# Second tap sums of a short convolution: from GpSimd's adder to adding transfers

## The chip, the cores and the metric

The kernel runs on one core of a Trainium2 chip. The metric is the device time of one execution in microseconds, the lower the better. The median of three runs before the change is 163.78 us (163.3 to 164.11).

## The reference

Two independent blocks are computed on sequences of 2048 positions and 576 channels, all in bf16, and their outputs are put side by side. Block A is a short convolution with four taps along the sequence, a product with `v`, a long convolution (by FFT) and a product with `q`. Block B is linear attention with 32 heads.

```python
def _A_ref(q, k, v, shift_k, ssm_k, ssm_D):
    B, S, D = q.shape
    ks = shift_k.shape[-1]                     # 4
    k_pad = jnp.pad(k, ((0, 0), (ks - 1, 0), (0, 0)))
    k_shift = jnp.zeros_like(k)
    for t in range(ks):
        k_shift = k_shift + k_pad[:, t:t + S, :] * shift_k[:, ks - 1 - t][None, None, :]
    kv = k_shift * v
    ...                                        # y = causal convolution of kv with ssm_k, by FFT
    y = y + kv * ssm_D[None, None, :]
    return q * y

def _B_ref(x, wqkv, wo):
    ...                                        # q, k, v = split of x @ wqkv into 32 heads of 18
    phi = lambda t: jnp.where(t > 0, t + 1, jnp.exp(t)) + 1e-6
    pq, pk = phi(q), phi(k)
    kv = jnp.einsum("bhsd,bhse->bhde", pk, v)
    z = jnp.einsum("bhsd->bhd", pk)
    num = jnp.einsum("bhqd,bhde->bhqe", pq, kv)
    den = jnp.einsum("bhqd,bhd->bhq", pq, z)[..., None] + 1e-6
    ...                                        # (num / den) merged over the heads, @ wo
```

## The kernel before

The long convolution is a discrete Fourier transform done in two stages of matrix products (`s1`, line 456, with the table `Gsb`; a 32x32 block transpose on VectorE, line 495; `s2`, line 504), a product in the frequency domain, and two stages back (lines 540 and 565). In block B, `kproj` (lines 604 to 612) and `qproj` (lines 625 to 631) project x and apply phi, with the results `pk` and `pqT`; line 654 forms x's product with `pk` over all positions, and line 794 makes the output.

The work around the change is the short convolution, `conv_piece`. Positions lie as 128 partitions of 16 consecutive positions; a piece is one third of the channels (192, `cc` = 0, 1, 2) and one half of the 16 positions (`bh` = 0, 1). So there are six pieces, in the order in which the program lists them: first all of what needs the first half of k, `kh0` (and v, `v0`), then the second half. For each piece a tile `m` of 128 x 4 x 8 x 192 elements is filled and folded:

- two tap products on VectorE (line 395), each making two of the four taps: 128 x 3072 elements, k times the tap weights `Wj`;
- the first tap sum, always on VectorE in this plan: m[0:2] += m[2:4], 128 x 3072 elements;
- the second tap sum, m[0] += m[1], 128 x 1536 elements;
- the product with v, written over v: 128 x 1536 elements.

The sums and the product go through the helper `tt`, so all have line 234 in the profile.

Nothing is scheduled at run time. The program's operations are listed once with their data dependences, and then issued in the order that a long string, `PLAN`, writes out; its letter names the engine of each operation (P TensorE, A ScalarE, D VectorE, G GpSimd, S the transfer queue of SyncE). A second string, `PLACES`, gives the place of every buffer in SBUF and PSUM, and buffers that are dead lend their places to others. Each engine runs its instructions in order; waits between engines follow from the buffers' places and the data. In this plan GpSimd has four of the six second tap sums, and behind the first two of them the product with v as well; VectorE has the other two sums and four products. Operations marked `two` that are given to GpSimd also wait for the last one of VectorE so marked:

```python
            if o.info.get("two"):
                if o.eng == "DVE":
                    last = ins
                elif last is not None:
                    tc.add_manual_dep(ins, last.name, ...,
                                      reason="products of VectorE and GpSimd one after the other")
```

The third piece writes its `m` where the second piece's was. The second half of k is loaded (1584 KB, SyncE's queue) once the last tap product that reads the first half is done. After each group of x the kernel makes a narrow copy `x<-x_sb` (line 231 on GpSimd, 229 on VectorE, 227 on ScalarE).

The prediction also speaks of three transfers of SyncE's queue (line 220): `X<-sph`, 256 KB from SBUF to SBUF for the product in the frequency domain; `r_scr<-rden`, 64 KB of reciprocal denominators into HBM; and `rb<-r_scr`, which reads them back, spread over partitions.

## Time and profile before

| | |
|---|---|
| runs before, median (lowest to highest) | 163.78 us (163.3 to 164.11) |
| the profiled execution, its time | 163.43 us |
| its span, from the first to the last instruction | 161.7 us |
| TensorE clock granted, mean | 0.997 |
| TensorE matmul busy | 153.7 us (95%) |
| VectorE busy | 145.1 us (90%) |
| ScalarE busy | 125.9 us (78%) |
| GpSimd busy | 55.9 us (35%) |
| second tap sums on GpSimd | 4 of 3.1 us, 12.4 us |
| second tap sums on VectorE | 2 of 0.96 us |

Busy time is the time in which at least one instruction of the engine was being worked on. In the profile PE is TensorE, DVE is VectorE, ACT is ScalarE, POOL is GpSimd, and SPq is SyncE's queue of transfers. The slices are 40 equal parts of the span, 4.04 us each, and a digit is the busy share in tenths. The chain that ended last is followed back from the last instruction, at each step to what released it. "Idle before" in a timeline is how long the engine had stood still, and what ended that. In the table of windows the columns are the stretch, its length, the busy time of PE, PEld (weight loads), DVE, ACT and POOL with the number of instructions, the granted clock, the mean busy share of the 16 transfer engines and the GB/s that they moved.

### The profile page before, as it was taken

What the parts mean: (1) busy time and instruction counts of PE and PEld (TensorE: products, weight loads), DVE (VectorE), ACT (ScalarE), POOL (GpSimd) and SP (SyncE); (2) the same over time, 40 slices, a digit from 0 to 9 for tenths busy, and PEclk for the clock granted to TensorE, in tenths of its full rate; (3) what the DMA queues carried; (4) which work ended last, traced back from release to release, by engine and by line L of the source; (5) the groups of instructions that cost most, each with busy time, mean ns of one, the idle gap of its engine ahead of it and who ended that gap; (6) DMA issues with size and microseconds to landing.
All of it is one profiled execution on the core that took longest, in us unless ns stands there. A gap on an engine that the chain in (4) does not pass through costs nothing.

```text
span 161.7 us, 4161 instructions
## 1 busy us (share of the span) xinstructions
PE 153.7 (95%) x1671; PEld 119.6 (74%) x1671; DVE 145.1 (90%) x173; ACT 125.9 (78%) x231; POOL 55.9 (35%) x50
## 2 busy tenths in 40 slices
PE   6899989999999999998999999999999999999991
PEld 2687877644645587896878887887578799999991
DVE  1319999997999999999999999999999999999790
ACT  3139989998988968878645469997999999989512
POOL 8603411110079277051001600999960000002900
PEclk9999999999999999999999999999999999999998
DMA  5999999999930800284940044489996597122975
GB/s 166 288 402 244 232 124 160 309 293 271 401 132 0 292 4 0 41 348 94 334 174 4 18 166 167 158 312 287 299 352 270 155 383 247 65 70 71 264 194 175
DMA packets 25135, 32.20 MB, mean 199 GB/s; under 512 B 15387, under 2 KB 20508, under 8 KB 24348
## 3 DMA queue, kind: packets, MB, share of 16 engines
q1 hardware_dynamic: 25116, 31.94, 65.6%
q8 instruction: 13, 0.21, 0.6%
q14 instruction: 6, 0.05, 0.1%
HBM read 20.27 MB, written 4.98 MB: 156 GB/s over the span
## 4 chain that ended last, share of the span: by engine, by line
PE 57%; DVE 17%; DMA 9%; ACT 5%; SPq 4%; POOL 4%; issue 3%; DVEq 0%; ACTq 0%
PE ps_all L794 13%; PE ps_all L540 10%; PE ps_all L625 10%; PE ps_all L654 6%; PE ps_all L456 6%; PE ps_all L565 5%; DMA hs<-in_A_ssm_k_dram 4%; PE ps_all L504 4%; DVE m L395 4%; DMA kh<-in_A_k_dram 4%; SPq L322 2%; DVE Ch L229 2%; DVE ct L495 2%; DVE rden L742 2%; DVE Cu L229 2%
## 5 line engine op out<-in xcount | busy, mean ns | idle before, releaser
L234 POOL TENSOR_TENSOR m<-m 128x1536 bf16<-128x1536 bf16 x4 | 12.4, 3102 | 34.7 <-DVE m L234 30.7
L625 PE MATMUL ps_all<-xT,wq 128*126 128x512 bf16 (+1 forms) x100 | 24.2, 380 | 0.0
L234 POOL TENSOR_TENSOR pqT<-pqT,rb 126x1024 bf16<-126x1024 bf16 (+1 forms) x9 | 18.9, 2125 | 9.5 <-DVE v L234 9.5
L794 PE MATMUL ps_all<-M,pqT 126*128 126x288 bf16 (+1 forms) x160 | 21.8, 286 | 0.3 <-DVE M L782 0.3
L604 PE MATMUL ps_all<-wk,xT 128*128 128x288 bf16 x160 | 20.7, 286 | 0.6 <-DMA wk<-in_B_wqkv_dram 0.6
L395 DVE TENSOR_TENSOR m<-kh,Wj 128x3072 bf16<-128x3072 bf16 x12 | 20.7, 1767 | 0.3 <-POOL v L234 0.2
L604 PEld LDWEIGHTS <-xT 128*128 128x128 bf16 x160 | 17.3, 110 | 4.0 <-issue 1.5
L456 PEld LDWEIGHTS <-Gsb 128*128 128x128 bf16 x192 | 16.1, 98 | 5.0 <-issue 2.8
L794 PEld LDWEIGHTS <-pqT 126*128 126x128 bf16 (+1 forms) x160 | 16.8, 109 | 3.7 <-issue 1.8
L227 ACT ACTIVATE sph<-ps_all 128x512 bf16<-128x512 f32 x30 | 16.6, 602 | 2.4 <-PE ps_all L504 2.3
L625 PEld LDWEIGHTS <-wq 128*126 128x126 bf16 (+1 forms) x100 | 12.4, 131 | 7.8 <-issue 1.8
L227 ACT ACTIVATE Cu<-ps_all 128x768 bf16<-128x768 f32 x20 | 16.2, 861 | 1.6 <-DVE m L395 0.8
L540 PE MATMUL ps_all<-Esb,sph 128*128 128x128 bf16 x144 | 17.2, 219 | 0.0
L540 PE MATMUL ps_all<-Esb,X 128*128 128x128 bf16 x144 | 17.1, 219 | 0.0
L654 PE MATMUL ps_all<-pk,x_sb 128*128 128x289 bf16 (+1 forms) x128 | 16.8, 287 | 0.0
L227 ACT ACTIVATE V<-ps_all 128x512 bf16<-128x512 f32 x26 | 14.9, 641 | 2.3 <-PE ps_all L540 2.1
L227 ACT ACTIVATE spu<-ps_all 128x512 bf16<-128x512 f32 x28 | 15.4, 619 | 0.6 <-PE ps_all L504 0.6
L609 ACT ACTIVATE ek<-ps_all,neg 128x576 bf16<-128x576 f32 x16 | 11.8, 747 | 4.4 <-PE ps_all L604 3.4
L227 ACT ACTIVATE Ch<-ps_all 128x768 bf16<-128x768 f32 x18 | 14.8, 853 | 0.5 <-PE ps_all L456 0.2
L227 ACT ACTIVATE ob<-ps_all 128x288 bf16<-128x288 f32 x30 | 11.7, 437 | 4.5 <-PE ps_all L794 4.0
L234 POOL TENSOR_TENSOR q<-yb,q 128x768 bf16<-128x768 bf16 x3 | 4.9, 1652 | 28.8 <-PE ps_all L565 28.8
L654 PEld LDWEIGHTS <-x_sb 128*128 128x128 bf16 x128 | 12.4, 98 | 3.0
(94 smaller groups left out, 313.3 us busy)
## 6 DMA issues: line engine op xcount, KB each, us to landing
X<-sph SPq DMA_DIRECT2D x18, 256.0 KB
x_sb<-in_B_x_dram SPq DMA_DIRECT2D x4, 576.0 KB
v<-in_A_v_dram SPq DMA_DIRECT2D x2, 1152.0 KB
out_dram<-ob SPq DMA_DIRECT2D x16, 144.0 KB
q<-in_A_q_dram SPq DMA_DIRECT2D x1, 2304.0 KB
out_dram<-q SPq DMA_DIRECT2D x12, 192.0 KB
rb<-r_scr SPq DMA_DIRECT2D x8, 252.0 KB
kh<-in_A_k_dram SPq DMA_DIRECT2D x1, 1584.0 KB
```

Source lines behind the costliest of these rows:

```text
L227: nc.scalar.activation(out=o, in_=i, func=ACTF.Copy)
L229: nc.vector.tensor_copy(out=o, in_=i)
L234: return (nc.vector if e == "DVE" else nc.gpsimd).tensor_tensor(out=o, in0=a, in1=b, op=op)
L395: return nc.vector.tensor_tensor(out=m.t[:, i:i + 2], in0=i0, in1=i1, op=ALU.mult)
L456: nc.tensor.matmul(ps.t[:, bank, lo - 384 * bank:hi - 384 * bank], lhsT=Gsb.t[:, b, ri, :], rhs=src[:, lo - CC * j:hi - CC * j], start=Tru ...
L540: nc.tensor.matmul(ps.t[:, 0, 128 * c:128 * c + 128], lhsT=src.t[:, 4 * hh + c, :], rhs=Esb.t[:, 32 + wi, :], start=(wi == 0), stop=(wi == 1))
L565: nc.tensor.matmul(ps.t[:, 0, n * j:n * j + n], lhsT=Esb.t[:, 2 * b + ri, :], rhs=V[gi].t[:, 2 * b + ri, :], start=(ri == 0), stop=(ri == 1))
L604: nc.tensor.matmul(ps.t[:, hh, 0:HALF], lhsT=cols(xT.t[0:KT[t], t, :], r), rhs=wk.t[0:KT[t], t, HALF * hh:HALF * hh + HALF], start=(t == 0 ...
L609: P.op("A", lambda e: nc.scalar.activation(out=eb.t[:], in_=ps.t[:, :, 0:HALF], func=ACTF.Exp, bias=neg1.t[:]), rd=[ps, neg1], wr=[eb], na ...
L625: nc.tensor.matmul(ps.t[0:hn, 0, :], lhsT=wq.t[0:KT[t], t, h0:h0 + hn], rhs=xT.t[0:KT[t], t, :], start=(t == 0), stop=(t == 4))
L654: nc.tensor.matmul(ps.t[0:m, 0, 0:n], lhsT=x4[r // 4].t[:, r % 4, :] if t == 4 else x_sb[r // 4].t[:, r % 4, 128 * t:128 * t + 128], rhs=p ...
L794: nc.tensor.matmul(ps.t[:, 0, 0:HALF], lhsT=cols(pqT[r // 8].t[0:kn, c, 512 * (r // 4 % 2):512 * (r // 4 % 2) + 512], r), rhs=M.t[0:kn, c, ...
```

## The change

The second tap sum of a piece that the plan gives to GpSimd is no longer an addition on GpSimd, but a transfer issued from GpSimd's queue, which reads m[1] from SBUF and adds it to m[0] in SBUF. The sums that the plan gives to VectorE stay as they are. `PLAN` and `PLACES` are unchanged, so every engine has the same operations in the same order, and each buffer lies where it lay.

```diff
-        P.op("DG", lambda e: tt(e, m.t[:, 0], m.t[:, 0], m.t[:, 1], ALU.add),
+        def add2(e):
+            if e == "POOL":
+                return nc.gpsimd.dma_start(out=m.t[:, 0].rearrange("p a c -> p (a c)"), in_=m.t[:, 1].rearrange("p a c -> p (a c)"), accum_op=ALU.add)
+            return tt(e, m.t[:, 0], m.t[:, 0], m.t[:, 1], ALU.add)
+        P.op("DG", add2,
              wr=[(m, 0)], name="tap+", n=1536, x2=1, two=1, st=st)
```

What waited for the addition now waits for the transfer's landing: GpSimd's product with v for the first two, VectorE's for the last two, and whatever takes the place of m.

## The prediction

> **What bounds the kernel now.** I read the busy table first, then the slices, the chain that ended last, and last the timelines of the engines around the four sums.

> ```profile
> span 161.7 us, 4161 instructions
> PE 153.7 (95%) x1671; PEld 119.6 (74%) x1671; DVE 145.1 (90%) x173; ACT 125.9 (78%) x231; POOL 55.9 (35%) x50
> DVE  1319999997999999999999999999999999999790
> POOL 8603411110079277051001600999960000002900
> ```

> TensorE and VectorE are both full: VectorE stands at 9 in nearly every slice from slice 10 (40 us) to slice 37 (152 us), and its timeline shows no idle time there longer than 0.22 us. GpSimd is busy for 35%. So GpSimd's own busy time is worth nothing; what counts is when its results come, and whether VectorE then stands still. A microsecond in which VectorE stands still before 152 us has almost nothing behind it to catch it up.

> The chain that ended last says where GpSimd sets the time (start, length, what):

> ```profile
> 57.46 3.12 POOL m L234
> 60.58 0.07 issue
> 60.65 3.11 POOL v L234
> 63.76 0.02 issue
> 63.78 3.44 DVE m L395 x2
> ...
> 67.35 5.95 DMA kh<-in_A_k_dram
> ```

> The second of the four sums is on it, then the product with v, then VectorE's next pair of tap products, which overwrite `m` and had waited 0.22 us; their end lets SyncE load the second half of k. The other three sums are seen in the timelines of GpSimd, VectorE and SyncE (start, length, engine, line):

> ```profile
> 45.27 3.10 POOL L234 TENSOR_TENSOR m<-m 128x1536 bf16<-128x1536 bf16 x1 [9.20 <-DVE m L234]
> 48.45 3.12 POOL L234 TENSOR_TENSOR v<-m,v 128x1536 bf16<-128x1536 bf16 x1
> 51.51 1.93 POOL L231 COPY x<-x_sb 128x256 bf16<-128x256 bf16 x1
> 51.43 1.75 DVE L395 TENSOR_TENSOR m<-kh,Wj 128x3072 bf16<-128x3072 bf16 x1
> 53.10 1.94 DVE L395 TENSOR_TENSOR m<-kh,Wj 128x3072 bf16<-128x3072 bf16 x1
> 70.35 3.11 POOL L234 TENSOR_TENSOR m<-m 128x1536 bf16<-128x1536 bf16 x1 [6.60 <-DVE m L234]
> 73.98 0.95 DVE L234 TENSOR_TENSOR v<-m,v 128x1536 bf16<-128x1536 bf16 x1
> 88.36 3.09 POOL L234 TENSOR_TENSOR m<-m 128x1536 bf16<-128x1536 bf16 x1 [14.91 <-DVE m L234]
> 92.20 0.90 DVE L234 TENSOR_TENSOR v<-m,v 128x1536 bf16<-128x1536 bf16 x1
> ```

> To be seen here: each sum takes 3.1 us. Behind the third and the fourth, VectorE does other work and reaches the product with v 0.52 us (73.98 - 73.46) and 0.75 us (92.20 - 91.45) after the sum is there. And GpSimd and VectorE exclude one another where both read two SBUF tiles: GpSimd's copy took 1.93 us, its twin at 5.48 us took 0.40; it ended at 53.44, just after the tap product of 51.43 to 53.18, and the next tap product, started at 53.10, took 1.94 instead of the median of 1.75.

> **The change, part by part.** Removed: four GpSimd additions of 3.1 us (12.4 us of GpSimd). Added: four transfers issued from GpSimd at the same places, each reading m[0] and m[1] (128 rows of 3072 B, 393 KB each) and writing m[0]. All engine orders and buffer places stay as they are. New waits: GpSimd's product with v waits for the transfer (first two), VectorE's product waits for it (last two), and VectorE's tap products of the third piece wait for the second transfer as well as for GpSimd.

> What does one such transfer take, from issue to release (call it L)? The trace has no transfer issued from GpSimd and none that adds, so I bound it by SyncE's:

> ```profile
> 91.38 0.55 SPq L220 DMA_DIRECT2D r_scr<-rden  x1
> 92.03 0.52 SPq L220 DMA_DIRECT2D X<-sph  x1
> 94.01 0.88 SPq L220 DMA_DIRECT2D rb<-r_scr  x1
> 93.25:93.75 0.50, 0.50 (x7) 0.39 (x5) 0.50 (x1) 0.42 (x2) 0.00 (x0) 1.00 1.08 415
> ```

> The load of `rb` had to wait for the 64 KB write of r_scr issued at 91.38 and went at 94.01: 2.6 us from issue to release for a small transfer, its 64 KB being 0.16 us of that at the 415 GB/s of the last row, so 2.45 us fixed. X (256 KB, SBUF to SBUF) was issued at 92.03 and its bytes had moved by 94.0. At 415 GB/s 393 KB take 0.95 us; the sum reads two such operands, so I count them twice, 1.9 us. Issuing takes SyncE 0.55 us; GpSimd, whose two-input add of 1536 elements is 3.1 us where VectorE's is 0.95, I let take twice that, 0.55 us more. L = 2.45 + 1.9 + 0.55 = 4.9, taken as 5.0 us. Lower bound: X's two microseconds and 0.3 us for its smaller size, 2.3 us. Upper bound: the k load, the longest in the chain (5.95 us, 1.6 MB, as if the sum moved four times its bytes), plus a GpSimd instruction of 2.1 us (its products with rb) for the issue: 8.1 us. I stay at 5.0, since the size is that of X and the fixed part that of r_scr; both ends go into the range.

> *First sum* (45.27). The product with v behind it ends at 51.57 + (5.0 - 3.1) = 53.5 instead of 51.57. VectorE wants to start the next tap products at 51.43; GpSimd's product, begun at 50.3, then has the tiles' port, and by the copy row VectorE waits for its end: 53.5 - 51.57 = **1.9 us**. What is behind it has room: GpSimd's copy and the next sum (4.0 us idle before it), and SyncE's x_sb load, issued right after the product at 51.59 and all moved by 56.4, whose row is needed by copies from 60.45 on. The price is L - 3.1 up to L = 6.1 and then stays near 3.1 us, because the product then starts behind one tap product and holds up the other.

> *Second sum* (57.46, after the VectorE sum and an ACT instruction that both end at about 57.4). On the chain: L - 3.1 = **1.9 us**, during which VectorE stands at line 395 with all the pk and pqT evictions behind it, and TensorE soon lacks PSUM banks. No transfer runs then (DMA share 0.00 from 58 to 68 us), so nothing slows it.

> *Third sum* (70.35). Room 0.52 us. It falls into the k load (share 1.03 at 70 to 72 us, 0.43 at 72 to 74 us). Its bytes start some 1.6 us after issue, so about 0.9 us of k's remain; sharing the engines with them costs the sum between 0 and 0.9 us, taken as 0.5, and k as much, which is hidden by the same stall. 5.0 + 0.5 - 3.1 - 0.52 = **1.9 us** before VectorE's product with v, with the last pk eviction queued behind it, for which TensorE's G products (line 654) wait.

> *Fourth sum* (88.36). Room 0.75 us, no transfer beside it until r_scr at 91.75. 5.0 - 3.1 - 0.75 = **1.15 us** before VectorE's product.

> What is saved: GpSimd time that nobody waits for, nothing. The sum is 1.9 + 1.9 + 1.9 + 1.15 = 6.85 us, all of it stall of VectorE in its full stretch. The profiled execution took 163.43 us (span 161.7 and 1.7 around it); 163.43 + 6.85 = 170.3. The median of the runs, 163.78, is 0.35 us above the profiled one, so I say 170.3 and leave that to the range.

> **Rivals.**
> *No change: the transfer is as quick as the addition.* With L at 3.1 or less every one of the four prices is nil: 163.4. At the lower bound of 2.3 us there is only the 0.22 us of VectorE's wait at 63.78 and the 0.19 us of the longer tap product to win: 163.0. So this ends on the other side without ever being a gain that can be measured (over 0.5%, 0.8 us, about what a measurement of this kernel can tell from no change). For it: X's bytes had moved within 2 us. Against it: r_scr's 2.6 us with a sixth of the bytes. The point where it decides is L = 3.4 us (0.3 + 0.3 + up to 0.3 + 0). Chance 0.11.
> [...]
> *The adding is slow.* If the transfer engines add well below their copy rate, or GpSimd takes long to write out 128 rows, L is 7 to 8 us: 3.1 + 4.9 + 4.9 + 4.25 = 17.2 at L = 8, 180.6; 13 to 14 at L = 7. For it: nothing in the trace shows adding at any rate. Chance 0.16.
> *No exclusion at the first sum.* If GpSimd's later product doesn't hold up the tap products (they only brushed in the trace before), the first price is nil: 168.4. Against it: both the copy and the tap product of the rows above were lengthened. Chance 0.07.

> **How the numbers follow.** The forecast (L between 3.4 and 7, all four prices) has 0.66. Slower is then 0.66 + 0.07 + 0.16, less a rest of 0.01 for L just above 3.4: 0.88. No change's 0.11 and that 0.01 make 0.12, of which I give 0.03 to a gain above 0.8 us by something not seen here and 0.09 to within 0.5%. The range: from L = 3.5 (0.4 + 0.4 + 0.4 + 0 = 1.2 us: 164.6) to L = 7.2, with 3.1 + 4.1 + 4.1 + 3.3 = 14.6: 178.0. It leaves out most of no change and the upper part of slow adding, together about 2 in 10.

> **What would show it.** VectorE's waits: before line 395's tap products at 51 us some 1.9 us behind GpSimd's product with v; before those at about 66 us some 2.1 us behind the same; before the products with v behind the third and the fourth sum 1.9 and 1.15 us for the transfer. GpSimd's busy time falls by 12 us less what issuing shows. VectorE's busy time stays at 145 us, its share falls. I am wrong if L lies outside 3.4 to 7 us, if the lost time is spread over TensorE with VectorE never waiting, or if the tap products at 51 us start on time though GpSimd's product runs beside them.

## The result, and the profile after

| | before | after |
|---|---|---|
| median of four runs each, one chip | 163.54 us (163.11 to 164.11) | 172.61 us (170.42 to 172.94) |
| after / before | | 1.052 (95%: 1.043 to 1.062) |
| the profiled execution | 163.43 us | 172.74 us |
| its span | 161.7 us | 171.0 us |

The change costs 9.1 us, 5.2%. The forecast was 170.3 us, with a range of 164.6 to 178.0. First the page of the changed kernel: span, busy times, and the slices of VectorE and of TensorE's granted clock (each slice is now 4.27 us).

```profile
span 171.0 us, 4169 instructions
PE 156.7 (92%) x1671; PEld 120.5 (71%) x1671; DVE 147.0 (86%) x173; ACT 126.0 (74%) x231; POOL 47.1 (28%) x50
DVE  1349999979999996993966999999999999999890
PEclk9999999999999999999579999999999999999999
```

GpSimd is 8.8 us less busy: 12.4 us of additions went, and 3.6 us of issuing came. VectorE has 2 us more busy time, nearly all of it one stretched tap product (below), and its share has fallen from 90% to 86%. Its row of nines now has holes, at slices 16, 19, 21 and 22. The last line has something that the prediction has no word of: in slices 20 and 21 (81 to 90 us) TensorE was granted only 0.5 and 0.7 of its clock.

The waits of VectorE between 60 and 105 us (what waited, for what, us in total, times, longest) show the holes:

```profile
DVE v L234 <- issue: 3.0, 1, 3.0
DVE zsel L714 <- PE ps_all L707: 2.9, 1, 2.9
DVE m L395 <- POOL v L234: 1.6, 1, 1.6
DVE v L234 <- DMA m<-m: 0.2, 1, 0.2
```

From the bottom: the fourth sum's product with v (0.2 us, waiting for the transfer), the tap products behind the second sum (1.6 us, waiting for GpSimd's product), `zsel` at 91 us (2.9 us, waiting for a matmul), and the third sum's product with v (3.0 us). The profile names no releaser for the last; the chain that ended last shows the adding transfer ahead of it:

```profile
59.32 3.97 DMA m<-m
...
73.47 3.32 DMA m<-m
76.79 2.98 issue
...
81.45 0.80 PE ps_all L460 x4
```

The third transfer is issued at 73.47 us, VectorE's product starts at 79.77 us, and TensorE comes back only at 81.45 us. The timelines of the engines around the sums (in brackets the idle time before, and what ended it):

```profile
49.93 3.08 POOL L234 TENSOR_TENSOR v<-m,v 128x1536 bf16<-128x1536 bf16 x1 [3.63 <-DMA m<-m]
50.97 3.65 DVE L395 TENSOR_TENSOR m<-kh,Wj 128x3072 bf16<-128x3072 bf16 x1
53.04 2.07 ACT L227 ACTIVATE sph<-ps_all 128x512 bf16<-128x512 f32 x4 [2.28 <-POOL v L234]
59.32 0.88 POOL L404 DMA_DIRECT2D m<-m  x1 [4.44 <-ACT eq L632]
81.45 0.80 PE L460 MATMUL ps_all<-v,Gsb 128*128 128x192 bf16 x4 [3.24 <-DVE pk L616]
```

The exclusion of the prediction is in the first two lines: a tap product of 3.65 us instead of 1.75 us, which ends 1.6 us after GpSimd's product does. The third line was not foreseen: ScalarE's copies `sph` take the place of the first `m`, and so waited 2.28 us for GpSimd's product too. The last line is TensorE's pause of 3.24 us at the third sum: the last `pk` eviction is queued on VectorE behind the product with v. Windows of 1 us (columns as before) show what follows:

```profile
82.00:83.00 1.00, 1.00 (x6) 0.63 (x5) 1.00 (x2) 0.00 (x0) 0.00 (x0) 0.50 0.92 256
88.00:89.00 1.00, 1.00 (x10) 0.79 (x9) 0.51 (x1) 0.00 (x0) 0.00 (x0) 1.00 0.00 0
```

At a granted clock of 0.50 TensorE finished 6 matmuls in the microsecond from 82 us, at 1.00 it finished 10 in that from 88 us.

Last, the transfer itself. All four, from the page of tile `m`, and the first of the eight quarter microseconds in which the second one's bytes move (60.75 to 62.75 us, all at 197 GB/s):

```profile
DMA to landing us min/median/max: 3.9/4.3/6.2
```

```profile
60.75:61.00 0.25, 0.25 (x4) 0.23 (x4) 0.25 (x1) 0.00 (x0) 0.00 (x0) 1.00 1.07 197
```

Issued at 59.32 us, first bytes 1.4 us later, 2.0 us of moving with all engines busy (share 1.07), landed 0.5 us after that: 3.97 us, where the addition took 3.12 us.

### The profile page after: what moved, and what is told of

It reads as the page before. It is cut to its first block, busy times and chain, and to the rows that moved or that the text cites. A ratio compares the mean times of both kernels' runs of the same rounds, so it can differ in the third digit from the quotient of the medians.

```text
span 171.0 us, 4169 instructions
## 1 busy us (share of the span) xinstructions
PE 156.7 (92%) x1671; PEld 120.5 (71%) x1671; DVE 147.0 (86%) x173; ACT 126.0 (74%) x231; POOL 47.1 (28%) x50
## 4 chain that ended last, share of the span: by engine, by line
PE 50%; DVE 21%; DMA 13%; ACT 5%; issue 4%; POOL 4%; SPq 0%; DVEq 0%; ACTq 0%; POOLq 0%
PE ps_all L798 12%; PE ps_all L544 9%; DMA m<-m 9%; PE ps_all L658 7%; DVE m L395 6%; PE ps_all L460 5%; PE ps_all L569 5%; PE ps_all L629 4%; POOL v L234 4%; DMA wk<-in_B_wqkv_dram 3%; PE ps_all L508 3%; DVE m L234 3%; DVE Ch L229 2%; DVE ct L499 2%; DVE pk L616 2%
## 5 line engine op out<-in xcount | busy, mean ns | idle before, releaser
L395 DVE TENSOR_TENSOR m<-kh,Wj 128x3072 bf16<-128x3072 bf16 x12 | 22.6, 1926 | 1.6 <-POOL v L234 1.6
L234 POOL TENSOR_TENSOR pqT<-pqT,rb 126x1024 bf16<-126x1024 bf16 (+1 forms) x9 | 18.9, 2127 | 12.5 <-DVE v L234 11.9
L629 PEld LDWEIGHTS <-wq 128*126 128x126 bf16 (+1 forms) x100 | 12.4, 131 | 7.9 <-issue 1.8
L544 PE MATMUL ps_all<-Esb,sph 128*128 128x128 bf16 x144 | 17.2, 219 | 0.0
L404 POOL DMA_DIRECT2D m<-m x4 | 3.6, 910 | 43.6 <-DVE m L234 29.8
L460 PE MATMUL ps_all<-v,Gsb 128*128 128x192 bf16 x96 | 11.2, 255 | 3.6 <-DVE pk L616 3.2
L658 PEld LDWEIGHTS <-x_sb 128*128 128x128 bf16 x128 | 12.4, 98 | 3.0
```

Source lines behind the costliest of these rows:

```text
L234: return (nc.vector if e == "DVE" else nc.gpsimd).tensor_tensor(out=o, in0=a, in1=b, op=op)
L395: return nc.vector.tensor_tensor(out=m.t[:, i:i + 2], in0=i0, in1=i1, op=ALU.mult)
L460: nc.tensor.matmul(ps.t[:, bank, lo - 384 * bank:hi - 384 * bank], lhsT=Gsb.t[:, b, ri, :], rhs=src[:, lo - CC * j:hi - CC * j], start=Tru ...
L544: nc.tensor.matmul(ps.t[:, 0, 128 * c:128 * c + 128], lhsT=src.t[:, 4 * hh + c, :], rhs=Esb.t[:, 32 + wi, :], start=(wi == 0), stop=(wi == 1))
L629: nc.tensor.matmul(ps.t[0:hn, 0, :], lhsT=wq.t[0:KT[t], t, h0:h0 + hn], rhs=xT.t[0:KT[t], t, :], start=(t == 0), stop=(t == 4))
L658: nc.tensor.matmul(ps.t[0:m, 0, 0:n], lhsT=x4[r // 4].t[:, r % 4, :] if t == 4 else x_sb[r // 4].t[:, r % 4, 128 * t:128 * t + 128], rhs=p ...
```

## The experiments

The theory: each transfer costs by its own lateness at its own place, and at the third place TensorE's lowered clock costs a further 3 us. Rivals: the cost is in equal shares, about 2.3 us for each sum; the lowered clock is only a companion of VectorE's stall, and costs nothing of its own; the third transfer is long because of k's load beside it, or because of something else.

### One sum at a time

```diff
-            if e == "POOL":
+            if e == "POOL" and (cc, bh) == (0, 0):      # e_first
```

with (1, 0), (2, 0) and (1, 1) for e_second, e_third and e_fourth; the other three sums stay additions on GpSimd.

> Only the first of the four sums is an adding transfer, the other three stay with GpSimd's adder. Theory (each sum costs what its own wait costs): the transfer takes about 4.6 us here, GpSimd's product with v ends some 1.4 us later than before, VectorE's tap products of the second piece are held up until its end; +1.3 to +1.9 us, 165 us. The later three sums stand as before, no stretch of lowered TensorE clock. Rival (every adding transfer costs about the same, a quarter of the 9 us): +2.3 us.

> Only the second sum is an adding transfer. Theory: it stands on the chain that ended last; transfer 4.0 us and 0.3 us later issue against 3.1 us of adding, +1.0 to +1.4 us, 164.8 us. Rival of equal shares: +2.3 us.

> Only the third sum is an adding transfer. Theory: it runs beside the load of the second half of k and takes about 6 us instead of 4, VectorE stands 3 us before the product with v, TensorE stands as long behind the last pk eviction, and its granted clock falls to 0.50 for some 6 us, which costs another 2.9 us: +5 to +6 us, 169 us; granted clock on average 0.98. Rival of equal shares: +2.3 us and no stretch of lower clock.

> Only the fourth sum is an adding transfer. Theory: transfer 3.9 us, issued 0.3 us after VectorE's sum; VectorE comes to the product with v 0.75 us after the adder would have been done, so +0.0 to +0.4 us, 163.7 us. Rival of equal shares: +2.3 us.

Measured against 163.49 us of the kernel before on the same chip:

| sum by transfer | median | more by | ratio (95%) | L, issue to landing |
|---|---|---|---|---|
| first | 165.32 us | 1.83 us | 1.011 (1.009 to 1.013) | 4.5 us |
| second | 165.20 us | 1.71 us | 1.010 (1.007 to 1.013) | 4.3 us |
| third | 168.03 us | 4.54 us | 1.028 (1.024 to 1.031) | 5.8 us |
| fourth | 164.64 us | 1.15 us | 1.009 (1.006 to 1.013) | 4.2 us |

The four make 9.23 us, the whole change 9.07 us. That they agree so closely is in part luck: by the shifts in the table further down, the third costs 1.4 us more in company than alone, and the second and the fourth together 1.3 us less. Equal shares fall: the third takes half. Of the four expectations the first was met; the second and the fourth came out dearer than expected (1.0 to 1.4 and 0.0 to 0.4 us), the third cheaper (5 to 6 us). The first transfer of each of these programs is also the only one, and as such it is slower: its issue takes 1.02 us against 0.86 to 0.88 us for the later ones of the changed kernel. In e_fourth the transfer begins 0.60 us after VectorE's sum and takes 4.2 us, in the changed kernel the fourth one begins 0.30 us after it and takes 3.9 us; so VectorE waits 0.80 us there instead of 0.18. The other 0.35 us of e_fourth's median are not explained: its profiled run took 164.19 us, and three of its ten runs took over 165.5 us.

### What the adding costs: copies instead

```diff
-in_=m.t[:, 1].rearrange("p a c -> p (a c)"), accum_op=ALU.add)
+in_=m.t[:, 1].rearrange("p a c -> p (a c)"))
```

> The four transfers copy m[1] over m[0] instead of adding it (the sum of the taps is left out); same bytes written, same waits. Theory: the adding reads both operands and takes 2.0 us of moving where a copy takes 1.0, so each transfer is 1.0 us shorter (2.9 to 3.0 us from issue to landing where nothing else runs), the first three prices fall by about 1 us each, and TensorE's pause of 3.2 us shrinks: 168 to 169.5 us. Rival (the time is all issue and landing, adding is free): no change from 172.6 us.

167.26 us against 163.37 us, 1.022 (1.016 to 1.028): 3.9 us more than before, where adding costs 9.1, and less than the 168 to 169.5 us expected. The landing times, from the page of tile `m`:

```profile
DMA to landing us min/median/max: 2.6/3.3/4.1
```

The second copy, with nothing beside it, took 2.64 us where the adding transfer took 3.97: issuing was 0.58 us instead of 0.88, and the bytes moved at 393 to 418 GB/s in 1.0 us instead of 197 GB/s in 2.0 us. So adding halved the rate here, as the prediction had it when it counted the operands twice. A transfer at copy speed would still not have paid here: at the third place it landed after 4.1 us, and the granted clock fell there too (to 0.50, from about 78 to 81 us), though TensorE had paused for only 1.18 us:

```profile
77.99 0.80 PE L460 MATMUL ps_all<-v,Gsb 128*128 128x192 bf16 x4 [1.18 <-DVE pk L616]
```

### Whether the lowered clock costs anything of its own

e_warm gives TensorE useless work in the pause, behind the operation after which it stood still; e_swap lets the last `pk` eviction (D107) go ahead of the product with v (D86), so that TensorE need not wait. All four sums are transfers in both.

```diff
# e_warm
             ins = o.fn(o.eng)
+            if o.id == 503:
+                for _ in range(12):
+                    nc.tensor.matmul(psall[:, 4, :], lhsT=Gsb.t[:, 0, 0, :], rhs=Gsb.t[:, 0:2]..., start=True, stop=True)
# e_swap, in PLAN
- D86 A528 P501 D107
+ D107 A528 P501 D86
```

> All four sums by adding transfers, and 12 matmuls of 512 columns without use (2.6 us) on TensorE in the pause behind the third sum, into a PSUM bank that is free then. VectorE's waits stay. Theory: the pause itself lowers the granted clock, and that costs 2.9 us of its own; with TensorE busy the clock stays at 1.00 and the time falls to 169.5 to 170.5 us. Rival (VectorE is the bound there anyway, the lower clock only goes along): 172.6 us or more.

> All four sums by adding transfers, and on VectorE the last pk eviction goes ahead of the third piece's product with v, so that it is not queued behind the third transfer. Theory: TensorE's G products start some 3 us earlier, no pause, granted clock 1.00, VectorE still stands 2.3 to 3 us: 169 to 170 us. Rival (the pk eviction behind the waiting product does not matter): 172.6 us.

e_warm took 170.34 us (1.042, 1.039 to 1.046), e_swap 169.71 us (1.040, 1.035 to 1.046), both as expected. They are 7.0 and 6.3 us above the kernel before on their chip, 2.1 and 2.7 us less than the changed kernel's 9.1. Their intervals meet that of the changed kernel (1.043 to 1.062), because one of its four runs took 170.42 us; the mean granted clock of that run was 0.99, that of the other three (172.47 to 172.94 us) 0.98. The granted clock is 1.00 at the place in both new programs. The `zsel` of the kernel before, and in e_warm's timeline the filling work and the `zsel`, which had waited 2.86 us in the changed kernel:

```profile
82.71 0.19 DVE L710 TENSOR_TENSOR zsel<-ps_all,cst 72x32 bf16<-72x32 f32 x1
78.66 2.54 PE L847 MATMUL ps_all<-Gsb 128*128 128x512 bf16 x11 [0.16 <-issue]
88.62 0.19 DVE L714 TENSOR_TENSOR zsel<-ps_all,cst 72x32 bf16<-72x32 f32 x1 [0.21 <-PE ps_all L707]
```

VectorE's wait at the third product is still 2.58 us there (3.00 in the changed kernel; the transfer took 5.8 us instead of 6.2), while the second wait has fallen from 2.86 to 0.21 us. e_swap's waits of VectorE look alike, without any added work:

```profile
DVE v L234 <- DMA m<-m: 2.2, 2, 2.0
DVE m L395 <- POOL v L234: 1.6, 1, 1.6
```

The stall for the transfer stays (2.04 us; the eviction that went ahead fills 0.76 us of the time), the wait for the matmul doesn't occur. e_swap alone doesn't part the clock from the pause, since TensorE also goes on earlier in it; e_warm does, since TensorE's own work starts as late as in the changed kernel (81.34 us against 81.45). So the lowered clock has a price of its own, and the rival falls. The price lies between 1.7 us (the 2.1 us of e_warm's median, less the 0.4 us by which its stall is shorter) and 2.65 us (by the wait at `zsel` in the profiled runs). The arithmetic gives the upper end: in the changed kernel TensorE worked at half rate from 81.45 to about 87.3 us, and half of 5.9 us is 2.9.

### Whether the first sum costs by GpSimd's lateness alone

e_late is the kernel before, without any transfer, but with a GpSimd `memset` of a dead part of `m` (1.38 us) ahead of the first product with v. e_place has the same instruction behind that product, so that the product itself is on time, and only what takes the place of `m` is late.

```diff
         def tapv(e):
+            if (cc, bh) == (0, 0):
+                nc.gpsimd.memset(m.t[:, 2], 0.0)        # e_late: ahead; e_place: behind the product
             return tt(e, vt.t[:, :, c0:c0 + CC], m.t[:, 0], vt.t[:, :, c0:c0 + CC], ALU.mult)
```

> The kernel before, all sums by GpSimd's adder, no transfer; ahead of the first product with v GpSimd fills a dead part of m (1536 elements, about 1.4 us), so that this product runs as late as behind the first transfer. Theory (the first sum costs only by the lateness of GpSimd's product, which holds up VectorE's tap products): +1.3 to +1.9 us, 165.1 us, and a tap product of 3.2 to 3.7 us. Rival (it is the transfer, its issue or its bytes, that costs): 163.5 us.

> The kernel before, all sums by GpSimd's adder; behind the first product with v, at its usual time, GpSimd fills a dead part of the first m (about 1.4 us, writing only), so that m's place comes free as late as behind the first transfer, while the product itself isn't late. ScalarE's sph evictions, which take that place, wait 1.4 us longer; the tap products do not meet a product of GpSimd. Theory (the lateness costs through the port that VectorE's tap products and GpSimd's product can't use together): 163.5 us. Rival (it costs through ScalarE's wait for the place of m): +1.2 us, 164.7 us. Both at once would lie between.

e_late took 164.66 us against 163.37, 1.008 (1.005 to 1.010). Its timeline, GpSimd's product with v and the two tap products:

```profile
49.98 3.11 POOL L234 TENSOR_TENSOR v<-m,v 128x1536 bf16<-128x1536 bf16 x1
51.75 4.82 DVE L395 TENSOR_TENSOR m<-kh,Wj 128x3072 bf16<-128x3072 bf16 x2
```

A late product alone costs 1.29 us, by a tap product of 2.95 us instead of 1.75. Counted from the end of VectorE's sum ahead of it, GpSimd's product starts after 3.32 us in the kernel before, after 4.52 us here and after 5.14 us in e_first: 1.20 us late costs 1.29 us, and 1.82 us late costs e_first's 1.83 us. (The product became less late than expected, and the tap product so shorter than the 3.2 to 3.7 us expected.) So the first sum's price is the lateness of GpSimd's product, whatever makes it late.

e_place was meant to tell the road through the tap products from the one through the place of `m`, and did so only in part. ScalarE's `sph` waited 1.71 us for the `memset`, as expected of that route; but the slightly moved order then met a new collision at the second product with v:

```profile
61.14 3.10 POOL L234 TENSOR_TENSOR v<-m,v 128x1536 bf16<-128x1536 bf16 x1
61.22 3.10 DVE L229 COPY x<-x_sb 128x256 bf16<-128x256 bf16 x1
```

VectorE's copy, 0.22 us long in the kernel before, starts 0.08 us behind GpSimd's product and lasts as long as that does. In the kernel before it starts at 60.45 us, 0.20 us ahead of the product. The runs spread from 164.66 to 168.34 us, neither of the two times expected, and no price can be read from them. The profiled run, up to that collision, does tell something: its pair of tap products takes as long as before (3.63 us against 3.62), VectorE then waits 0.55 us for ScalarE's `eq`, and ends the sum behind it (line 234, ahead of the second transfer's place) 0.63 us later than before. So the road through the place of `m` alone is worth about 0.6 us at this point. In the changed kernel it adds nothing to the first sum's price: VectorE has no wait for ScalarE there, and the lengthening of its tap product (3.65 - 1.75 = 1.9 us) is the whole loss.

### Why the third transfer took 6.2 us

e_khold has only the third sum by transfer, and the load of the second half of k is held back until that transfer has landed.

```diff
# PLAN: S60, the load of kh1, moved from its place to behind G85, the third sum
+            if o.id == 85:
+                third = ins
+            if o.id == 60:
+                tc.add_manual_dep(ins, third.name, ..., reason="k behind the third sum")
```

> Only the third sum by an adding transfer, and the load of the second half of k, with the loads behind it, is issued after that transfer has landed. Theory (the third transfer is long because it shares the transfer engines with k, v and X): 4.2 us from issue to landing instead of 5.8; the kernel itself becomes slower, since k comes 4 to 5 us later. Rival (it is long for another reason, such as VectorE's work beside it): 5.8 us as before.

170.91 us (1.047, 1.044 to 1.050): the late k costs VectorE 4.85 us at its next tap products, as such a kernel must. What counts is L: 5.13 us, with no load beside it, against 5.8 us in e_third and 4.2 us in e_fourth, each of them the first such transfer of its program. So neither theory nor rival (4.2 and 5.8 us) was right by itself. Two quarter microseconds out of its windows show what holds it up, and the transfer queues between 72.5 and 75.8 us (packets, MB, share of 16 engines) name it:

```profile
73.25:73.50 0.25, 0.25 (x4) 0.21 (x3) 0.25 (x2) 0.00 (x0) 0.00 (x0) 1.00 1.23 250
74.75:75.00 0.25, 0.16 (x8) 0.00 (x0) 0.00 (x0) 0.25 (x1) 0.00 (x0) 1.00 0.07 12
```

```profile
q8 instruction: 1, 0.02, 1.8%
```

At 73.25 us one packet of an instruction load comes between (250 GB/s instead of 197). From 74.75 to 75.75 us the transfer then runs at 12 GB/s and a share of 0.06 to 0.07, which is one of sixteen engines: fifteen are done, and one is about 1.1 us behind. The same peak is in the changed kernel (262 GB/s at 76.0 us) and in e_third (262 GB/s at 73.25 us). So of the 1.6 us by which e_third's transfer is longer than e_fourth's, about 0.7 us is k's load (5.8 - 5.13) and about 0.9 us (5.13 - 4.2) the one late engine. The traces' single packets fit the instruction load as what made it late. In five programs such a packet falls into the third adding transfer: it takes 0.90 us in e_third, 0.98 in e_khold, 1.11 in e_warm, 1.48 in the changed kernel and 1.60 in e_swap, and the last engine ends 0.8, 1.1, 0.9, 1.4 and 1.5 us behind the other fifteen. The second and the fourth transfers of the changed kernel, with no such packet among theirs, end within 0.03 us on the last two engines. The profile doesn't show which engine a packet was on, and no run took the load away.

## Why the prediction was right, and where its sum was wrong

The prices by place. "Shift" is how much later VectorE does the same thing in the changed kernel than before, less what was already lost: the end of VectorE's sum ahead of the first of the four (45.13 to 44.67 us, so the profiled run of the changed kernel is 0.46 us ahead there, before anything is changed), the end of the pair of tap products behind the first sum (55.04 to 56.49 us), the start of the next pair (63.78 to 66.50), the product behind the third sum (73.98 to 79.77), `zsel` (82.71 to 91.36), the product behind the fourth sum (92.20 to 101.12), the end of the span.

| step | predicted | shift | alone |
|---|---|---|---|
| up to the first sum | none | -0.5 us | |
| first sum | 1.9 us | 1.9 us | 1.8 us |
| second sum | 1.9 us | 1.3 us | 1.7 us |
| third sum, VectorE's stall | 1.9 us | 3.1 us | 4.5 us, with the next row |
| third sum, lowered clock | none | 2.9 us | |
| fourth sum | 1.15 us | 0.3 us | 1.15 us |
| the rest to the end | none | 0.4 us | |
| sum | 6.85 us | 9.3 us | 9.2 us |

That the fourth sum alone costs just the 1.15 us foretold is chance; in the changed kernel it costs 0.3 us.

**L.** Predicted 5.0 us, measured 4.6, 4.0, 6.2 and 3.9. The moving term (1.9 us, each operand counted once at 415 GB/s) was right: 2.0 us. The rest was too large: 2.45 us fixed and 0.55 us for GpSimd's slower issue were 3.0 us, and 1.9 us are seen (1.4 until the first byte, 0.5 behind the last, at the second sum). The fixed part was taken from r_scr by a wrong reading: the prediction let its 64 KB move at 415 GB/s, in 0.16 us, but that rate is the one of X's bytes. Before these, in the kernel before, r_scr's moved at a fifth of it:

```profile
92.25:92.50 0.25, 0.25 (x4) 0.20 (x2) 0.25 (x2) 0.00 (x0) 0.00 (x0) 1.00 0.29 84
```

At 84 GB/s 64 KB take 0.8 us, so that some 1.85 us would have been left as the fixed part (an estimate from this row). And no run shows the 0.55 us for GpSimd's slower issue as a term beside the 1.9 us. The prediction's point of decision, L = 3.4 us, was passed by all four, by 0.5 us at the least.

**A start that was not counted.** GpSimd begins to issue a transfer 0.60, 0.54 and 0.30 us after the VectorE sum that it waits for (the first, third and fourth: 44.67 to 45.27, 72.93 to 73.47, 96.88 to 97.18); the addition before began 0.14 us after it (45.13 to 45.27). At the second sum the start is 0.42 us later than the shift up to there accounts for (57.46 + 1.44 = 58.90 against 59.32). With it the second price is 0.42 + 3.97 - 3.12 = 1.27 us, as measured, and the first, which came out at the forecast's 1.9 us, did so by luck: an L that was 0.4 us too long stood against a start that was missed by 0.46 us.

**First and second sum.** Mechanism and place as foretold: the exclusion (3.65 us instead of 1.75; it shows as a longer tap product, not as the wait that was to be seen before it) and VectorE's wait at line 395 (1.58 us; 2.1 foretold). The rival that the tap products aren't held up falls. The row that the exclusion was read from is a GpSimd copy, which reads one tile and not two; what held VectorE up here is GpSimd's product, which reads two. No run shows a port that the two engines share, of which the prediction and e_place's expectation speak; the runs show the times, a tap product of 3.65 us here and of 2.95 us in e_late instead of 1.75. A second road, ScalarE's wait for the place of `m`, was missed; it cost VectorE nothing here.

**Third sum.** This is the term that was mis-sized: 1.9 us foretold, 3.1 + 2.9 measured. L was to be 5.0 + 0.5 us here and was 6.2, with k's load beside it, v's and wo's loads behind that, and an instruction load that the prediction did not look for. The 1.6 us from its issue to its first bytes were the author's estimate; they came 2.1 us after it (73.47 to 75.54). And the prediction named the wait of line 654's G products (658 now) for the last `pk` eviction, but put no price on TensorE standing still: behind a pause of 3.24 us its granted clock was 0.50 for 5.9 us of work, and with the pause filled, in e_warm, 1.00.

**Fourth sum.** 0.2 us of wait instead of 1.15 us, since L was 3.9 us and the room 0.75 us.

So the total was within 2.3 us partly by luck, because two terms were too large by 1.5 us together (0.6 and 0.9) and one was too small by 4.1 us. Direction and range rested on L above 3.4 us at four places with little room, and that held. Of the rivals, "no change" and "the adding is slow" (7 us and more) both failed by L. (In the latter's sum at L = 8 the fourth term should be 8 - 3.1 - 0.75 = 4.15 us, not 4.25; nothing else changes by it.)

## What to carry to other kernels

Work moved off an engine that was a third busy won nothing by itself here (GpSimd 8.8 us less busy, the whole 9.1 us longer); ask how long the result takes from the last input to the first reader. Here an addition of 3.1 us became a transfer of 3.9 us at best, on a path with 0.0 to 0.75 us of room. And where TensorE waits behind somebody else's wait, count its pause: pauses of 1.2 to 3.2 us were followed by half the clock here, in the changed kernel at a price of about 2 us, and letting the eviction that it needs go first, as e_swap did, won that back.
